# Three sealed experts, the last pair before expert work, V loaded once, and the zero fill spread over the pairs

## Chip, cores, metric

The kernel runs on one core of a Trainium2 chip. The metric is the device time in microseconds; the page and the trace come from one profiled execution, whose times are counted from its first instruction. The engines are named PE (matmul), PEld (its weight loads), DVE or VectorE, ACT or ScalarE, POOL or GpSimd, and SP or SyncE, which here only issues DMAs.

## What is computed

Attention in chunks over 4 batches, 8 heads, 768 positions, head size 64, then a top-2 mixture of 8 experts on the 3072 resulting rows of 512.

```python
for c in range(nc):                      # 24 chunks of 32 positions
    l_start = max(0, c_start - 16); r_end = min(S, c_end + 8)
    k_full = concat(mem_k, k[l_start:r_end]); v_full = concat(mem_v, v[l_start:r_end])   # 8 memory rows
    a = softmax(scale * q_c @ k_full.T); out[c] = a @ v_full
x = out as [3072, 512]
noisy_logits = x @ w_gate + log1p(exp(x @ w_noise)) * noise
top2, weights = the two largest of 8, softmax over them
for e in range(8): out[rows that chose e] += weight * (relu(x @ w1[e]) @ w2[e])          # 512 -> 1024 -> 512
```

## The kernel before

**Attention** runs over 16 pairs of heads (four pairs to a batch) in one software pipeline: iteration i of the main loop holds the steps of pairs i - 3 to i + 2. For a pair, q and k are turned by PE (`turn_pe`, copied out by ACT), scored (`scores_pe`), the maximum is taken off by VectorE (`max_dve`), ACT takes the exponent (`exp_act`), PE turns the result (`PT_pe`, copied by ACT in `PT_copy`), multiplies it with V (`PV_pe`), and VectorE normalises (`mult_dve`) into `xrows[b]`, a tile with all rows of batch b in two rotating buffers. `xT_pe` and `logits_pe` give the routing logits. q and k are loaded six pairs ahead. V is loaded three pairs ahead into four buffers `vbufs` (`load_v`): a chunk's window of 56 positions (16 left, 32 own, 8 right) lies on 56 partitions, so of 24 windows each position at an edge is loaded twice or more. These loads are issued by GpSimd, as they convert to bf16.

**Routing** of batch b (`route(b)`, steps s1 to s8) starts when the batch's logits are there: s1 the noise scale on ACT; s1b and s2 all-pairs comparison on VectorE; s2b, s2c masks and maxima; s2d exponent on ACT; s3 on PE the rank of each token in its expert, counted on from `seen`; s4 the weights and the store of `xrows[b]` to the DRAM tensor `x_rows` (SP's queue for batches 0 to 2, ACT's for 3); s4b, s5 slot and tile; s5c `col` on GpSimd; s5b `Rn` on VectorE; s6 the table by matmul; s7 adds the table of the batch before; s8 counts `seen` on. The steps of batches 0 to 2 are dealt out to the loop through `pending`, one group at each call of `steps`.

**Sealed slots.** Each expert has 7 tiles of 128 slots (the last 64). For the first EARLY experts, tiles 0 and 1 are filled from batches 0 and 1 alone, and tiles 2 and 3 from batches up to 2: in s8 the count is raised to the border (`gap`), and free slots are given to spare rows (`spare_a` to `spare_d`). So these tiles' tokens can be gathered before the last batch is routed: `begin_first` decodes the table after batch 1 and gathers tiles 0 and 1 (`idx_s`), after batch 2 follow tiles 2 and 3 (`idx_a`); everything else waits for the last table (`idx_f`, and `idx_h` for the half tiles).

**Expert work** is a generator, `every`: sets of an expert's tiles, in the order: the sealed tiles of the early experts in two halves (`part`: turn two tiles, then `up` over 256 slots), their `down`, then the remaining three tiles of each early expert, then the full experts. `gather` fetches a tile's rows by an indirect DMA of GpSimd; `turn` transposes them on PE; `up` is x @ w1 with ReLU on ACT and VectorE; `down` multiplies with w2, scales by the gate and scatters the result with addition into the output by an indirect DMA of GpSimd. The first scatter of a set waits for the landing of the whole set before it. Weights come in three buffers each, loaded by GpSimd between gathers and scatters. `units(k)` runs k steps of the generator between other work; `until` runs the rest.

In before, `every` starts in the main loop's iteration 15 and interleaves with the last pair (the loop has a 17th turn for it) and with the routing of batch 3. The output is zeroed by three DMAs on SP's queue after the loop.

The engines' queues are in program order, each engine on its own: an instruction that waits holds back everything behind it on its engine.

Of the kernel before, what the change touches and what calls it, by code (L numbers as in the profile page):

```python
# [12 lines left out]
F32 = mybir.dt.float32  # L13
BF16 = mybir.dt.bfloat16
# [10 lines left out]
def kernel(  # L25
# [14 lines left out]
    nc = tc.nc  # L40
# [12 lines left out]
    HP = H // 2  # L53
# [35 lines left out]
    def body():  # L89
# [27 lines left out]
        NQ = 6  # L117

        NV = 4
        vbufs = [ap_.tile([128, ncnk, 2, D], BF16, name=f"vp{i}", bufs=1) for i in range(NV)]  # L120

        def load_qk(n):
            b, h0 = divmod(2 * n, H)
# [4 lines left out]
        def load_v(n):  # L128
            vp = vbufs[n % NV]
            for hh in range(2):  # L130
                p0, hd = 64 * hh, 2 * n + hh

                def piece(c, m, j=0, nj=WIN):
                    nc.gpsimd.dma_start(  # L134
                        out=vp[p0 + j:p0 + j + nj, c:c + m, hh, :],
                        in_=bass.AP(v.tensor, v.offset + (hd * S + c * chunk + j - left_ctx) * D, [[D, nj], [chunk * D, m], [1, D]]))

                first, last = hd == 0, hd == B * H - 1
                if first:
                    piece(0, 1, left_ctx, WIN - left_ctx)  # L140
                if last:
                    piece(ncnk - 1, 1, 0, WIN - right_ctx)
                piece(int(first), ncnk - first - last)

        load_qk(0)
        identb = const.tile([128, 128], BF16, name="identb")
# [163 lines left out]
        def PV_pe(n):  # L310
            PT, vp = st[n]["PT"], vbufs[n % NV]
            pv = bankO[:, :, :UB * 2 * OW].rearrange("p x (u h c) -> p x u h c", h=2, c=OW)
            for u in range(BT):
                nc.tensor.matmul(out=pv[:, u // UB, u % UB], lhsT=PT[:, u, :], rhs=memv[:, n], start=(u % UB == 0), stop=False, skip_group_check=True)  # L314
            for c in range(ncnk):
                u, r = divmod(c, 4)
                nc.tensor.matmul(out=pv[32 * r:32 * r + 32, u // UB, u % UB, :, :D], lhsT=PT[:, u, 32 * r:32 * r + 32],  # L317
                                 rhs=vp[:, c], start=False, stop=True, skip_group_check=True)
            st[n]["po"] = pv

        def mult_dve(n):
# [32 lines left out]
        def route(b):  # L354
# [61 lines left out]
            def s4():  # L416
                ge, gs = R["ge"], T("gs", [128, BT])
                nc.vector.tensor_mul(ge, ge, R["two"])
# [3 lines left out]
                (nc.sync if b < B - 1 else nc.scalar).dma_start(out=xd_part[b][b * S:(b + 1) * S].rearrange("(t p) r -> p t r", p=128), in_=xrows[b])  # L422

            def s4b():
                sh = [128, BT, 2, E]
# [46 lines left out]
            def s8():  # L472
                if b == B - 1:
                    return
                sm = T("sm", [128, E])
                nc.vector.tensor_reduce(out=sm, in_=R["two"].rearrange("p t e -> p e t"), axis=AX, op=Alu.add)
# [4 lines left out]
                if b >= B - 3:  # L481
# [6 lines left out]
                    nc.vector.tensor_add(seen[:, :EARLY], seen[:, :EARLY], gap)  # L488

            if b == B - 1:  # L490
                return (s1,), (s1b, s2), (s2b, s3, s2c, s4b, s5, s5c), (s2d,), (s4, s5b), (s6, s7)
# [120 lines left out]
        def turn(s, j):  # L612
            e, tiles = sets[s]
            if s not in xTs:
                small = len(tiles) < NT
                xTs[s] = (mp if small else pools["full"]).tile([128, KP, SEALED * CAP if small else SLOTS], BF16, name="xTs" if small else "xTf", bufs=2)
                gts[s] = mp.tile([128, NT], F32, name="gt", bufs=4)
# [17 lines left out]
        def up(s, c0=0, c1=None):  # L635
            e, tiles = sets[s]
            c1 = total(s) if c1 is None else c1
            if s not in hts:
                small = len(tiles) < NT
                hts[s] = (mp if small else pools["full"]).tile([128, FB, SEALED * CAP if small else SLOTS], BF16, name="hts" if small else "htf", bufs=2)  # L640
            k = -(-(c1 - c0) // 512)
            for f in range(FB):
                for c in range(k):
                    h = hring[cnt["h"] % 3] if hring else tr()
# [46 lines left out]
        def every():  # L691
# [11 lines left out]
            def load(fn, e):  # L703
                return (lambda: fn(e),) if e < E else ()

            yield from down(0, load(load_w1, EARLY))
            gather(2 * EARLY, ALL, idx_f, load(load_w2, EARLY))
            yield from down(1)
            for s in range(EARLY, NS):
                e = sets[s][0]  # L710
                while todo and todo[0][0] <= s:
# [4 lines left out]
                        turn(*todo.pop(0))  # L716
                yield from up(s)
                if s == EARLY:
                    gather(2 * EARLY + 1, ALL, idx_f, load(load_w1, e + 3))
                elif s < NS - 1:  # L720
                    todo.extend((s + 1, j) for j in sets[s + 1][1])
                    yield from down(s - 1, load(load_w1, e + 3))
                    more = load(load_w2, sets[s - 1][0] + 3)
                    if s + 3 < NS:
                        gather(s + 3, ALL, idx_f, more)
                    else:
                        for fn in more:
                            fn()
# [26 lines left out]
        for i in range(NPAIR + 1):  # L755
            if i + NQ < NPAIR:
                load_qk(i + NQ)
            if i >= 1:
                PT_pe(i - 1)
            if i < NPAIR:  # L760
                max_dve(i)
            if i >= 1:
                PT_copy(i - 1)
            if i + 2 < NPAIR:
                turn_pe(i + 2, 0)
            if i < NPAIR:
                steps(1)
            if i >= 1:
                PV_pe(i - 1)
            if i < NPAIR:  # L770
                exp_act(i)
            if i >= 3:
                logits_pe(i - 3)
                if (i - 3) % HP == HP - 1:
                    begin, *rest = route((i - 3) // HP)
                    begin[0]()
                    assert not pending
                    pending.extend(rest)
# [4 lines left out]
            if i >= 2:  # L783
                xT_pe(i - 2)
            if i + 1 < NPAIR:
                scores_pe(i + 1)
# [6 lines left out]
            if i == NPAIR - 4:  # L793
                load_w1(1)
            if i == NPAIR - 2:
                load_w2(0)
            steps(1 if i < NPAIR - 2 else 2)
            if i >= NPAIR - 1:
                units(FB // 2)
        assert not pending  # L800
        pctx.close()
# [11 lines left out]
        logits_pe(NPAIR - 2)  # L813
        xT_pe(NPAIR - 1)
        cnt["by"] = "dve"
        for j in range(FIRST):
            turn(1, j)
        logits_pe(NPAIR - 1)
        begin, *rest = route(B - 1)
        begin[0]()  # L820
        units(3)
        cnt["by"] = "act"
        for g, more in zip(rest, (3, 4, 1, 4, 1)):
            for fn in g:
                fn()
            units(more)
# [135 lines left out]
```

## Time and profile before

| | us |
|---|---|
| median of 3 runs (342.05 to 343.34) | 343.24 |
| profiled execution | 343.07 |
| its span, first to last instruction | 341.3 |
| busy: PE / DVE / ACT / POOL | 274.3 / 161.2 / 149.5 / 229.3 |
| mean granted TensorE clock | 0.918 |

The span has three stages. Attention lasts to about 95, with the maximum of pair 12 at 79.45 and of pair 15 at 101.34. From there to 145 the last pair, the last routings and the first expert work share the engines. From 145 to 324 the experts run; the scatters and their landing end at 341.3. An idle time in brackets is what the engine waited before an instruction, and what ended the wait by the trace; "issue" is time in which it waited for nothing that the profile shows.

### The profile page before, as it was taken

To read this page: it belongs to the slowest core of one execution; us is meant where nothing else is said; L and a number is where in the kernel's file an instruction comes from. 1 tells how busy PE (TensorE), PEld (TensorE's weight loads), DVE (VectorE), ACT (ScalarE), POOL (GpSimd) and SP (SyncE) were. 2 spreads that over 40 slices of the span, in tenths; PEclk is the share of its full clock that TensorE was granted. 3 is DMA by queue.
4 is the path that set the end of the run, shared out by engine and by line. 5 is a ranking of instruction groups with operands and counts; after the bars stand their busy time and mean duration, and the time that the engine had idled before them with its cause. 6 is when DMAs were issued, how large, how long until landed. Compare 5 with 4: busy or idle time off the path is not lost. (4 is left out here: it accounts for less than half of the span.)

```text
span 341.3 us, 7625 instructions
## 1 busy us (share of the span) xinstructions
PE 274.3 (80%) x3071; PEld 174.2 (51%) x3085; DVE 161.2 (47%) x363; ACT 149.5 (44%) x295; POOL 229.3 (67%) x219
## 2 busy tenths in 40 slices
PE   0777677878548667799999999999999999999900
PEld 0656566666436555345565555555555555455400
DVE  7457659779876465222434333342332633134100
ACT  1688988878355544123343433423423333132200
POOL 8997767737443250687788887887888784848281
PEclk9969978969695999899999999999999999999965
DMA  9999999999979999469999999999999999959395
GB/s 108 161 154 187 167 161 166 212 133 194 196 143 309 398 286 203 79 103 185 247 152 198 172 240 197 239 195 194 206 160 205 216 148 157 147 74 130 40 131 70
DMA packets 99110, 60.30 MB, mean 177 GB/s; under 512 B 63488, under 2 KB 83968, under 8 KB 99072
## 3 DMA queue, kind: packets, MB, share of 16 engines
q0 software_dynamic: 82208, 49.84, 106.5%
q1 hardware_dynamic: 15792, 9.05, 9.2%
q10 hardware_dynamic: 1072, 0.88, 0.8%
q8 instruction: 26, 0.43, 0.5%
q14 instruction: 12, 0.10, 0.1%
HBM read 65.07 MB, written 23.27 MB: 259 GB/s over the span
## 5 line engine op out<-in xcount | busy, mean ns | idle before, releaser
L676 POOL DMA_INDIRECT out_dram<-ys,idx_f x40 | 62.8, 1570 | 26.6 <-issue 14.8
L648 PEld LDWEIGHTS <-w1t 128*128 128x128 bf16 x576 | 56.3, 99 | 40.4 <-issue 5.1
L604 POOL DMA_INDIRECT xl<-x_rows,idx_f x48 | 50.0, 1041 | 26.7 <-DVE hts L633 11.2
L664 PE MATMUL bankE<-w2t,htf 128*128 128x512 bf16 x278 | 65.7, 379 | 0.5
L675 DVE TENSOR_SCALAR ys<-bankE,gt 128x512 f32<-128x512 f32 (+1 forms) x32 | 21.9, 684 | 63.3 <-PE bankE L664 49.8
L648 PE MATMUL bankE<-xTf,w1t 128*128 128x416 bf16 x256 | 50.6, 339 | 0.0
L673 ACT ACTIVATE ys<-bankE,gt 128x512 f32<-128x512 f32 x24 | 16.5, 688 | 68.1 <-PE bankE L664 59.3
L134 POOL DMA_DIRECT2D vp<-in_v_dram x34 | 33.4, 989 | 15.5 <-PE bankO L317 4.3
L664 PEld LDWEIGHTS <-htf 128*128 128x128 bf16 x288 | 27.2, 98 | 28.8 <-issue 0.2
L633 DVE TENSOR_SCALAR htf<-bankE 128x416 bf16<-128x416 f32 x32 | 18.9, 591 | 26.7 <-PE bankE L648 26.7
L631 ACT ACTIVATE htf<-bankE 128x416 bf16<-128x416 f32 x32 | 16.5, 517 | 27.1 <-PE bankE L648 27.1
L264 ACT COPY kT<-bankT 64x768 bf16<-64x768 bf16 x32 | 25.3, 791 | 6.5 <-PE bankT L254 6.2
L648 PE MATMUL bankT<-xTf,w1t 128*128 128x416 bf16 x128 | 27.8, 339 | 0.2 <-DVE htf L633 0.2
L621 PE MATMUL bankT<-identb,xl 128*128 128x128 bf16 (+1 forms) x224 | 20.5, 220 | 5.7 <-DMA xl<-x_rows,idx_f 2.4
L621 PEld LDWEIGHTS <-xl 128*128 128x128 bf16 (+1 forms) x224 | 15.4, 100 | 16.2 <-issue 4.4
L664 PE MATMUL bankE<-w2t,hts 128*128 128x512 bf16 x92 | 22.7, 395 | 0.2
L288 DVE TENSOR_REDUCE mx<-bankS 128x12 f32<-128x768 f32 x16 | 15.2, 953 | 9.1 <-PE bankS L283 9.1
L314 PE MATMUL bankO<-memv,PT 128*128 128x132 bf16 x96 | 10.2, 256 | 9.5 <-ACT PT L307 9.3
L648 PE MATMUL bankE<-xTs,w1t 128*128 128x256 bf16 (+1 forms) x104 | 14.9, 283 | 2.6 <-DVE xTs L625 1.3
L456 POOL TENSOR_TENSOR col<-mm_all,tl 128x672 f16<-128x672 f16 x4 | 6.7, 1672 | 14.6 <-DVE tl L443 14.6
L329 DVE TENSOR_TENSOR xrow<-bankO,rec 128x768 bf16<-128x768 f32 x16 | 15.3, 958 | 1.9 <-DMA x_rows<-xrow 1.4
L290 DVE TENSOR_TENSOR sd<-bankS,mx 128x768 f32<-128x768 f32 x16 | 15.3, 958 | 1.8 <-DVE mx L288 0.5
(182 smaller groups left out, 453.6 us busy)
## 6 DMA issues: line engine op xcount, KB each, us to landing
w1t<-in_moe_w_dram POOLq DMA_DIRECT2D x8, 1024.0 KB, 11.3
w2t<-in_moe_w_dram POOLq DMA_DIRECT2D x8, 1024.0 KB, 10.7
out_dram<-zt SPq DMA_DIRECT2D x3, 2048.0 KB, 10.2
vp<-in_v_dram POOLq DMA_DIRECT2D x30, 168.0 KB, 8.6
qg<-in_q_dram POOLq DMA_DIRECT2D x16, 192.0 KB, 7.7
kg<-in_k_dram POOLq DMA_DIRECT2D x16, 192.0 KB, 8.2
x_rows<-xrow SPq DMA_DIRECT2D x3, 792.0 KB, 8.4
x_rows<-xrow ACTq DMA_DIRECT2D x1, 792.0 KB
```

What stands on the lines that cost most here:

```text
L134: nc.gpsimd.dma_start(out=vp[p0 + j:p0 + j + nj, c:c + m, hh, :], in_=bass.AP(v.tensor, v.offset + (hd * S + c * chunk + j - left_ctx) * D ...
L264: nc.scalar.copy(kbufs[n % 2][hs, hh].rearrange("d (p j) -> d p j", j=SJ), p_t[hs])
L290: nc.vector.tensor_tensor(out=sd, in0=st[n]["ps"], in1=mx.rearrange("p x (u o) -> p x u o", o=1).to_broadcast([128, 2, BT, CTX]), op=Alu.s ...
L604: nc.gpsimd.indirect_dma_start(out=xl, out_offset=None, in_=xd, in_offset=bass.IndirectOffsetOnAxis(ap=idx[:, c:c + 1], axis=0), bounds_ch ...
L621: nc.tensor.transpose(out=p_t[:, kp, :w], in_=xl[:w, kp * 64:(kp + 1) * 64].bitcast(BF16), identity=identb[:w, :w])
L631: nc.scalar.activation(out=dst, in_=src, func=Act.Relu)
L633: nc.vector.tensor_scalar(out=dst, in0=src, scalar1=0.0, scalar2=None, op0=Alu.max)
L648: nc.tensor.matmul(out=h[:, :hi - lo], lhsT=W1[e][:, kp, f * 128:(f + 1) * 128], rhs=xTs[s][:, kp, lo:hi], start=(kp == 0), stop=(kp == KP ...
L664: nc.tensor.matmul(out=y, lhsT=ht[:, f, o:o + w], rhs=W2[e][:, f, :], start=(f == 0), stop=(f == FB - 1))
L673: nc.scalar.activation(out=ys[:, :wide], in_=y[:, :wide], func=Act.Copy, scale=gate)
L675: nc.vector.tensor_scalar(out=ys[:, :wide], in0=y[:, :wide], scalar1=gate, scalar2=None, op0=Alu.mult)
L676: ins = nc.gpsimd.indirect_dma_start(out=rows, out_offset=bass.IndirectOffsetOnAxis(ap=idx, axis=0), in_=ys[:, :wide], in_offset=None, bou ...
```

## The change

- EARLY goes from 2 to 3: experts 0, 1 and 2 have sealed tiles, with three buffers for their turned rows and hidden values; sets are 11 instead of 10, and the order of gathers, weight loads and turns in `every` is adapted. W1 of expert 2 is loaded in pair 14, W1 of expert 1 in pair 11 instead of 12.
- `up` over 256 slots puts two blocks of 128 hidden units into one PSUM bank and evacuates both at once.
- The raising of the counts moves from s8 into a step s8b; for batch 1, s8 comes one group earlier.
- V is loaded once: 32 own positions of each chunk, as one contiguous row per partition; the left and right edges are then copied inside the SBUF by four DMAs of SP's queue a pair, which wait for the load.
- The zero fill is done in eight DMAs of SP's queue, in pairs 1 to 8, behind that pair's copies.
- The main loop ends with iteration 15. The steps of the last pair follow it, with the routing of batch 2 between them; expert work starts after the last pair's logits, in three portions of four units between the steps of the routings of batches 2 and 3. Batch 3's store goes to SP's queue.

```diff
-    EARLY = 2
+    EARLY = 3
...
         def load_v(n):
             vp = vbufs[n % NV]
             for hh in range(2):
-                p0, hd = 64 * hh, 2 * n + hh
...
+                p0, hd = 64 * hh + left_ctx, 2 * n + hh
+                nc.gpsimd.dma_start(
+                    out=vp[p0:p0 + chunk, hh],
+                    in_=bass.AP(v.tensor, v.offset + hd * S * D, [[D, chunk], [chunk * D, ncnk], [1, D]]))
+
+            for hh in range(2):
+                p0 = 64 * hh
+                nc.sync.dma_start(out=vp[p0:p0 + left_ctx, hh, 1:], in_=vp[p0 + chunk:p0 + chunk + left_ctx, hh, :ncnk - 1])
+                nc.sync.dma_start(out=vp[p0 + left_ctx + chunk:p0 + WIN, hh, :ncnk - 1], in_=vp[p0 + left_ctx:p0 + left_ctx + right_ctx, hh, 1:])
...
-                (nc.sync if b < B - 1 else nc.scalar).dma_start(out=xd_part[b]...
+                nc.sync.dma_start(out=xd_part[b]...
...
-                return (s1,), (s1b, s2), (s2b, s2c, s2d), (s3, s4, s4b, spare_a), (s5, s5c, spare_b), (s5b, spare_c), (s6, s7, s8, spare_d, begin_first)
+                return (s1,), (s1b, s2), (s2b, s2c, s2d), (s3, s4, s4b, spare_a), (s5, s5c, spare_b), (s5b, spare_c, s8), (s6, s7, s8b, spare_d, begin_first)
...
+            if 2 * w <= 512:
+                for f in range(0, FB, 2):
+                    h = hring[cnt["h"] % 3] if hring else tr()
...
+                    relu(hts[s][:, f:f + 2, c0:c1], h[:, :2 * w].rearrange("p (x w) -> p x w", w=w))
+                    yield "up", s, f
+                return
...
+            if 1 <= i <= 8:
+                zero_fill(NP // 8 * (i - 1), NP // 8)
...
+        n = NPAIR - 1
+        r2 = late[B - 2]
+        PT_pe(n)
+        PT_copy(n)
+        xT_pe(n - 2)
+        do(r2, "s1b", "s2")
+        PV_pe(n)
+        mult_dve(n)
+        logits_pe(n - 3)
+        xT_pe(n - 1)
+        logits_pe(n - 2)
...
+        do(r2, "s2b", "s2c")
+        xT_pe(n)
+        do(r2, "s3", "s4b", "s8")
+        logits_pe(n - 1)
+        turn(0, 0)
+        logits_pe(n)
+        r3 = route(B - 1)
+        do(r3, "s1")
+        do(r2, "s2d")
+        turn(0, 1)
+        do(r2, "s5", "s5c", "s8b", "s5b", "s4")
+        units(4)
+        do(r2, "s6", "s7")
         decode(tabs[(B - 2) % 2][:, :EARLY * NT], idx_a, None)
         for s in range(EARLY):
             gather(s, range(FIRST, SEALED), idx_a)
-        for x in range(3):
-            zero_fill(8 * x, 8)
         load_w2(1)
...
+        do(r3, "s1b", "s2", "s2b", "s2c")
+        units(4)
+        do(r3, "s3", "s4b", "s2d", "s5", "s5c", "s4", "s5b")
+        units(4)
+        do(r3, "s6", "s7")
...
         decode(tab, idx_f, idx_h)
         for s in range(EARLY, 2 * EARLY):
             gather(s, sets[s][1], idx_f)
-            todo.extend((s, j) for j in sets[s][1])
+        load_w2(2)
```

More of the change, by code (lines that the diff above doesn't have):

```diff
@@ L119, in body @@
         NV = 4
-        vbufs = [ap_.tile([128, ncnk, 2, D], BF16, name=f"vp{i}", bufs=1) for i in range(NV)]
+        vbufs = [ap_.tile([128, 2, ncnk, D], BF16, name=f"vp{i}", bufs=1) for i in range(NV)]
         def load_qk(n):
@@ L480, in s8, with s8b @@
                     nc.vector.tensor_copy(seen, sm)
-                if b >= B - 3:
+            def s8b():
+                if B - 3 <= b < B - 1:
                     ps_c = f32v(tr(), EARLY)
@@ L639, in up @@
                 small = len(tiles) < NT
-                hts[s] = (mp if small else pools["full"]).tile([128, FB, SEALED * CAP if small else SLOTS], BF16, name="hts" if small else "htf", bufs=2)
+                hts[s] = (mp if small else pools["full"]).tile([128, FB, SEALED * CAP if small else SLOTS], BF16, name="hts" if small else "htf", bufs=EARLY if small else 2)
             k = -(-(c1 - c0) // 512)
+            w = c1 - c0
+            if 2 * w <= 512:
+                for f in range(0, FB, 2):
+                    h = hring[cnt["h"] % 3] if hring else tr()
+                    cnt["h"] += 1
+                    for x in range(2):
+                        for kp in range(KP):
+                            nc.tensor.matmul(out=h[:, x * w:(x + 1) * w], lhsT=W1[e][:, kp, (f + x) * 128:(f + x + 1) * 128], rhs=xTs[s][:, kp, c0:c1],
+                                             start=(kp == 0), stop=(kp == KP - 1))
+                    relu(hts[s][:, f:f + 2, c0:c1], h[:, :2 * w].rearrange("p (x w) -> p x w", w=w))
+                    yield "up", s, f
+                return
             for f in range(FB):
@@ L704, in load @@
                 return (lambda: fn(e),) if e < E else ()
-            yield from down(0, load(load_w1, EARLY))
-            gather(2 * EARLY, ALL, idx_f, load(load_w2, EARLY))
-            yield from down(1)
+            for s in range(EARLY):
+                yield from down(s)
+                if s < EARLY - 1:
+                    for t in (EARLY,) if s == 0 else range(EARLY + s, 2 * EARLY):
+                        todo.extend((t, j) for j in sets[t][1])
             for s in range(EARLY, NS):
@@ L754, in body @@
                 scores_pe(0)
-        for i in range(NPAIR + 1):
+        late = {}
+        for i in range(NPAIR):
             if i + NQ < NPAIR:
@@ L782, in body @@
                 mult_dve(i - 1)
-            if i >= 2:
+            if 2 <= i < NPAIR - 1:
                 xT_pe(i - 2)
```

79 lines of the change are left out of this document (30 added, 49 removed).

## The prediction

> **What bounds the kernel now.** I read the table by stretches first, then GpSimd's timeline, then the groups, then the one place where VectorE waits for a DMA. The page's span line and four rows of the table by stretches (length; busy time and count of PE, PEld, DVE, ACT, POOL; granted clock; DMA share; GB/s):
>
> ```profile
> span 341.3 us, 7625 instructions
> 25.00:45.00 20.00, 15.09 (x408) 12.28 (x404) 12.61 (x18) 18.04 (x24) 14.43 (x17) 0.93 1.79 176
> 45.00:65.00 20.00, 14.96 (x371) 11.89 (x372) 16.92 (x37) 15.91 (x24) 15.07 (x17) 0.88 1.97 183
> 105.00:115.00 10.00, 7.04 (x87) 5.31 (x86) 4.90 (x13) 5.08 (x11) 2.76 (x1) 0.68 1.07 376
> 145.00:285.00 140.00, 137.68 (x891) 76.60 (x901) 51.93 (x102) 48.63 (x127) 111.14 (x90) 1.00 1.06 189
> ```
>
> In the attention stage (25 to 65) ACT is nearest to full (18.04 of 20 us), VectorE joins it once a batch is being routed (16.92), and DMA is busy in short pieces: 176 to 183 GB/s, where the zero fill of the output, nearly alone from 105 to 115, moves 376. In the expert stage PE is 98% busy, and GpSimd's 111 us hide gaps that its timeline shows (start, duration, idle before):
>
> ```profile
> 138.35 1.13 POOL L604 DMA_INDIRECT xl<-x_rows,idx_f  x1 [11.25 <-DVE hts L633]
> 285.93 1.59 POOL L676 DMA_INDIRECT out_dram<-ys,idx_f  x1 [4.74 <-DMA out_dram<-ys,idx_h]
> 302.67 1.55 POOL L676 DMA_INDIRECT out_dram<-ys,idx_f  x1 [4.03 <-DVE ys L675]
> 321.92 1.55 POOL L676 DMA_INDIRECT out_dram<-ys,idx_f  x1 [6.54 <-issue]
> 333.07 1.55 POOL L676 DMA_INDIRECT out_dram<-ys,idx_h  x1 [0.30 <-issue]
> L676 POOL DMA_INDIRECT out_dram<-ys,idx_f x40 | 62.8, 1570 | 26.6 <-issue 14.8 <-DMA out_dram<-ys,idx_h 4.7 <-DVE ys L675 4.3
> L604 POOL DMA_INDIRECT xl<-x_rows,idx_f x48 | 50.0, 1041 | 26.7 <-DVE hts L633 11.2 <-issue 9.4 <-PE bankT L621 1.2
> L557 POOL DMA_DIRECT2D w1t<-in_moe_w_dram x8 | 9.5, 1191 | 0.0
> L562 POOL DMA_DIRECT2D w2t<-in_moe_w_dram x8 | 8.4, 1053 | 0.0
> ```
>
> From 138.35 GpSimd issues without rest: a gather is 1.04 + 0.30 = 1.34 us, a scatter 1.57 + 0.30 = 1.87. 48 gathers (64.3), 56 scatters (104.7) and 12 weight loads (about 13.5) are 182.5; with the three waits (15.3, a set's first scatter waiting for the landing of the set before) that is 197.8, against 196.3 in the trace up to the last scatter's end at 334.62. Its landing ends the span. So GpSimd's queue sets the end, with PE close behind. Two numbers matter: the start S of the gathers by the final index table (138.35), and what is left for GpSimd and PE at S. S itself waits for data:
>
> ```profile
> 129.65 0.41 ACTq L422 DMA_DIRECT2D x_rows<-xrow  x1
> 133.83 0.23 DVE L549 TENSOR_SCALAR idx_h<-idx_f,halfc 128x8 int32<-128x8 int32 x1
> DMA to landing us min/median/max: 5.6/8.4/10.7
> ```
>
> The table is ready at 134; the store of the last batch's rows, issued at 129.65 (third row: all such stores), lands near 138. All sums below are made against the profiled execution: 343.07 us, 1.8 above its span and 0.2 below the median of the runs, 343.24.
>
> **The change part by part.** *Work ahead of S.* With three sealed experts 12 tiles instead of 8 are gathered before S, and one more W1 is loaded ahead: 4 x 1.34 + about 1.0 = 6.4 us leave GpSimd's queue after S. **-6.4.** The scatters stay 56.
>
> *What PE still owes at S.* Before S PE now does three of six half parts; the other three stand between the last table and the first down tile.
>
> ```profile
> 132.43 0.72 PE L621 MATMUL bankT<-identb,xl 128*128 128x128 bf16 x8
> 137.95 1.89 PE L664 MATMUL bankE<-w2t,hts 128*128 128x512 bf16 x7
> 150.54 7.08 PE L664 MATMUL bankE<-w2t,hts 128*128 128x512 bf16 x32
> L675 DVE TENSOR_SCALAR ys<-bankE,gt 128x512 f32<-128x512 f32 x24 | 18.0, 751 | 49.8 <-PE bankE L664 49.8
> ```
>
> One half part (turn two tiles, 32 matmuls) is 137.95 - 132.43 = 5.5 us, so three are 16.5. The table's last matmul lies 2.3 before S (below), so down starts at S + 14.2 and its first result is there at S + 14.2 + 1.9 + 0.75 = S + 16.8. GpSimd is ready at S + 9 gathers + one W2 = S + 13.4. It waits 3.4. Over the 12 tiles of these sets PE is as fast as GpSimd or a little slower: a tile is 7.08 / 4 = 1.77 against 1.87 for its scatter, but nine turns at 0.36 (half of the first row) lie between, so 0 to 2.1 more; I take 1. **+4.4.** Cover: none, since GpSimd sets the end. Evacuating two blocks of up at once (512 columns) I cost at nothing: a quarter of a half part gives 1.4 us for an evacuation that takes about 0.75 (last row); without that cover it would be the difference, four times a half part.
>
> *From the last pairs to S.* Now attention runs to its end, and the routings of batches 2 and 3 follow in turn. I count from the end of mult_dve(12), the normalisation of pair 12, which in before is at 93.29 (45.06 before S):
>
> ```profile
> 67.80 0.95 DVE L288 TENSOR_REDUCE mx<-bankS 128x12 f32<-128x768 f32 x1
> 92.33 0.96 DVE L329 TENSOR_TENSOR xrow<-bankO,rec 128x768 bf16<-128x768 f32 x1
> 98.41 0.20 DVE L369 TENSOR_TENSOR nl<-ns,nz_all 128x48 f32<-128x48 f32 x1
> 101.22 0.21 DVE L398 TENSOR_TENSOR gd<-nl,m 128x48 f32<-128x48 f32 x1
> 103.20 0.20 DVE L418 TENSOR_TENSOR ge<-ge,two 128x48 f32<-128x48 f32 x1
> 104.02 0.25 DVE L427 TENSOR_TENSOR rk<-mm_all,bankT 128x96 f32<-128x96 f16 x1
> 105.32 0.24 DVE L432 TENSOR_REDUCE r_all<-rk 128x12 f32<-128x96 f32 x1
> 106.66 1.75 DVE L450 TENSOR_TENSOR Rn<-rampm,slot 128x1536 f16<-128x1536 f16 x1
> 114.38 0.23 DVE L476 TENSOR_REDUCE sm<-two 128x8 f32<-128x48 f16 x1
> 115.59 0.16 DVE L488 TENSOR_TENSOR seen<-seen,gap 128x2 f16<-128x2 f16 x1
> 82.88 1.31 POOL L456 TENSOR_TENSOR col<-mm_all,tl 128x672 f16<-128x672 f16 x1 [1.38 <-DVE tl L443]
> 131.35 0.48 PE L463 MATMUL bankT<-col,Rn 128*128 128x56 f16 x12 [0.21 <-DVE Rn L450]
> ```
>
> VectorE has, up to the store of batch 2: two max-and-subtract pairs of two 0.96 steps (4.1), three normalisations (3.6), s1b to s2c (98.41 to 101.43: 3.0), s4 (0.8), rk (0.25), s5 (1.3), Rn (1.75), s8 and s8b (1.3): 16.1, and about 1 of waiting for PE and ACT. The store goes at +17 and lands at +24 (7, between 5.6 and 8.4). Six gathers wait for it: 8.0; then W2(1), 1.0 + 0.3; then batch 3's col, which stands behind these on GpSimd, 1.3; the table's matmuls 0.5; table and decoding 2.0 (131.83 to 133.83) + 0.3. Sum +37.4, against 45.06. **-7.7.** Batch 3's store is issued near +29 and lands inside that.
>
> *V once, copies and zero fill on SP.* A pair's V writes fall from 336 to 192 KB. Two chains grow. First, SP now waits for V to land before it copies its edges, and what stands behind waits too: the zero fill of the pair, and the store x_rows of batch 0 (issued in pair 7, after load_v(10)) and of batch 1 (pair 11, after load_v(14)). The xrow buffers are two, so mult_dve(8) and mult_dve(12) wait for those stores:
>
> ```profile
> 54.22 1.99 POOL L134 DMA_DIRECT2D vp<-in_v_dram  x2 [0.26 <-PE bankT L254]
> DMA to landing us min/median/max: 5.8/8.5/11.1
> 56.15 48.34 SPq L422 DMA_DIRECT2D x_rows<-xrow  x3
> 76.43 0.83 PE L317 MATMUL bankO<-vp,PT 128*32 128x128 bf16 x24
> 66.93 0.96 DVE L329 TENSOR_TENSOR xrow<-bankO,rec 128x768 bf16<-128x768 f32 x1 [1.39 <-DMA x_rows<-xrow]
> 77.58 1.98 POOL L134 DMA_DIRECT2D vp<-in_v_dram  x2 [3.18 <-PE bankO L317]
> 137.76 0.37 SPq L850 DMA_DIRECT2D gov<-x_rows  x1
> ```
>
> Already now the store of batch 0, issued at 56.15, holds mult_dve(8) until 66.93. After: V(10)'s second half is issued at 55.1 and lands at 62.6 (7.5, between least and median, as it is smaller); two copies and the zero fill issue first (three times 0.4), so the store goes at 63.8; the zero fill ahead of it takes 0.79 MB / 376 GB/s = 2.1, the store 8.4: 74.3. That is 7.4 later. From here to mult_dve(12) a pair takes (92.33 - 66.93) / 4 = 6.35, and in the next one VectorE itself needs 2.05 + 1.2 + 1.5 (half of s1b to s2c) = 4.75, so 1.6 comes back. **+5.8.** V(14): 78.5 + 7.5 + 0.8 + 6.5 (no zero fill ahead any more) = 93.3 against 92.33: **+1.0.** PV itself has room: V(10), issued at 54.22, is read at 76.43. Bounds: with least landings (55.1 + 5.8 + 1.2 + 2.1 + 5.6 = 69.8) the first costs 1.3 and the second nothing; with the largest (80.2; 101.1) 11.7 and 8.8. I stay near the middle.
>
> Second, 8 x 2.1 = 17 us of zero fill enter a stage whose DMA is busy, against 144 KB less V a pair, which at 183 GB/s is 0.8 us, 6 over the eight pairs. The net 11 us are a debt that the loads can carry: V has 22 us from issue to use and needs 11.1 at most, so 11 are free there, and q and k run six pairs ahead. The upper bound, with a third of it felt, is +4. The lower is -4: ACT idles 2 of 20 us in 25 to 45, and loads that come sooner can win no more than that over the loop's 40 us from 25. I take 0, between the two. In exchange the stretch after 105 is free of the fill.
>
> The Trainium skill, DMA: Bandwidth & Descriptors, section Issuing engines are not separate DMA queues, speaks against this part: whatever the issuing engine, all DMAs share the same 16 engines and interleave, so SP's queue adds no bandwidth. If by that rule none of the fill found room, the sum would be 17 higher. The trace agrees that the queues share (the store of batch 0 took 10.8 us to release its buffer beside loads, against 5.6 at the least), but it has no fill beside loads.
>
> **Sum:** -6.4 + 4.4 - 7.7 + 6.8 = -2.9: 343.07 - 2.9 = **340.2**.
>
> The skill's TensorE: Matmul & The Clock Gate, section What's actually happening, has a matmul clock that falls to half after an idle window of about 3.4 us and needs as long to return; PE would wait about 3 us for col before the last table, so the half parts would start at half speed: +1.7 by an estimate from that page, within my near sides. The trace agrees in kind: the granted clock is 0.68 in 105 to 115.
>
> **The rivals.** *A, slower: the stores held on SP decide.* Place: mult_dve(8) and mult_dve(12). For it: the stage's DMA is loaded (1.97) and now gets the zero fill, so landings near 11 rather than 8 are likely. Against: V is lighter. Midway between my value and the largest, the two cost 13.7 instead of 6.8: 347.1. The time is worse than before once they cost more than 9.7 together. *B, faster: the held stores cost little.* With least landings 1.3, and loads coming 1 sooner: 333.7. For it: less V traffic, and no zero fill beside the gathers of batch 2. *C, the routing does not get ahead:* six gathers stand in front of batch 3's col, and if batch 2's store takes 10.7 instead of 7, S comes 3.7 later: 343.9, no change. Against: zero fill is out of that stretch.
>
> **How the numbers follow.** About 0.5%, 1.7 us, is what a measurement of this kernel can tell from no change. Chances: my forecast with its near sides (336 to 341.3) 0.32; B 0.22; C 0.16; A 0.30. Faster 0.54, same 0.14 (C mostly), slower 0.32 (A and C's upper part). The range leaves out 0.1 on each side: 332 (B with another 1.5 from less DMA) to 349 (A with 2 more). The likely case alone spans 336 to 344.
>
> **What would show it.** In the new profile: mult_dve(8) with 8 to 9 us of waiting for x_rows in pair 9 and about 1 in pair 13; 15 to 18 us from mult_dve(12) to s4 of batch 2; the first idx_f gather about 37 us after mult_dve(12), near 137; 44 gathers behind it without rest; a first scatter that waits for ys. I am wrong if mult_dve(8) does not wait, if the attention loop itself is slower per pair in 30 to 60, or if GpSimd rests in the expert stage.

## The result, and the profile after

The changed kernel takes 365.8 us (median of 4 runs, 364.7 to 369.1) against 342.6 for the kernel before on the same chip: a ratio of 1.070, 95% interval 1.062 to 1.078. It is 7% slower where 0.8% faster was forecast, and beyond the upper end of the range, 349. The profiled execution took 364.7 us, 1.7 above its span of 363.0; the span is 21.7 longer than before.

The path of the prediction has three stretches. In the profiled executions:

| | before | forecast change | measured change |
|---|---|---|---|
| end of mult_dve(12) | 93.29 | +6.8 | +13.1 (106.41) |
| from there to S, the first idx_f gather | 45.06 | -7.7 | +3.1 (48.2) |
| from S to the end of the span | 202.95 | -6.4 + 4.4 | +5.5 (208.4) |

All three came out longer. The first, in VectorE's timeline (start, duration, idle before and its releaser):

```profile
59.53 0.96 DVE L325 TENSOR_TENSOR xrow<-bankO,rec 128x768 bf16<-128x768 f32 x1
78.87 0.96 DVE L325 TENSOR_TENSOR xrow<-bankO,rec 128x768 bf16<-128x768 f32 x1 [13.97 <-DMA x_rows<-xrow]
105.45 0.96 DVE L325 TENSOR_TENSOR xrow<-bankO,rec 128x768 bf16<-128x768 f32 x1 [2.41 <-DMA x_rows<-xrow]
```

Up to mult_dve(7) the loop keeps the pace of before (59.53 against 60.38). Then mult_dve(8) idles 14 us for the store of batch 0, where it waited 1.39 before. In the windows by stage (PE, PEld, VectorE, ACT, GpSimd busy, then clock, DMA share and GB/s) VectorE stands still for the whole stretch from 65 to 75. The GB/s at the ends of the first two rows are against 167 and 163 before:

```profile
35.00:45.00 10.00, 7.75 (x213) 6.07 (x211) 6.22 (x9) 8.51 (x12) 5.86 (x9) 1.00 1.42 275
45.00:55.00 10.00, 7.38 (x212) 5.84 (x209) 8.33 (x17) 8.42 (x15) 5.09 (x8) 1.00 1.42 262
65.00:75.00 10.00, 1.54 (x51) 1.33 (x48) 0.00 (x0) 3.85 (x6) 1.44 (x2) 0.71 1.40 281
```

SP's queue in the same place: the edge copies wait for V(10), which was issued near 53, then take 0.53 and 0.66 us each to issue; the fill and the store follow.

```profile
65.00 0.53 SPq L138 DMA_DIRECT2D vp<-vp  x1
65.59 0.66 SPq L139 DMA_DIRECT2D vp<-vp  x1
66.36 0.53 SPq L138 DMA_DIRECT2D vp<-vp  x1
66.93 0.66 SPq L139 DMA_DIRECT2D vp<-vp  x1
67.63 0.44 SPq L575 DMA_DIRECT2D out_dram<-zt  x1
68.57 0.38 SPq L418 DMA_DIRECT2D x_rows<-xrow  x1
```

The V loads' own answer for 35 to 72 gives their time to landing, which was 7.9/8.9/10.6 before, for 168 KB a load instead of 96:

```profile
DMA to landing us min/median/max: 8.4/10.5/15.4
```

The second stretch, in the timelines of GpSimd, VectorE and SP:

```profile
131.44 1.11 POOL L602 DMA_INDIRECT xl<-x_rows,idx_a  x1 [10.55 <-DVE rk L423]
133.40 0.21 DVE L417 TENSOR_TENSOR xrow<-ge,gs 128x48 f32<-128x48 f32 x1
139.10 1.01 POOL L602 DMA_INDIRECT xl<-x_rows,idx_a  x1 [0.30 <-issue]
140.10 0.97 POOL L560 DMA_DIRECT2D w2t<-in_moe_w_dram  x1
142.08 0.37 SPq L418 DMA_DIRECT2D x_rows<-xrow  x1
154.59 1.11 POOL L602 DMA_INDIRECT xl<-x_rows,idx_f  x1 [12.17 <-DMA x_rows<-xrow]
```

and a line of SP's waits (total, times, longest):

```profile
SPq L418 <- DMA xl<-x_rows,idx_a: 17.9, 3, 11.7
```

Batch 3's rows are ready at 133.6, but their store is issued at 142.08: it waits until the idx_a gathers, which read the same DRAM tensor, have landed. Behind W2(1) it then needs 12 us more, and S waits for that. In the kernel before, the last of these gathers was issued at 120.88 and the four took 6.3 to 7.6 us to land, so all had landed before the last store was due (129.65). The dependency cost nothing there and I passed it over.

The third stretch, the first scatters of the sealed sets, and the end; the first row is the first scatter of set 1 in the kernel before, where seven gathers stood ahead of it:

```profile
166.40 1.63 POOL L676 DMA_INDIRECT out_dram<-ys,idx_a  x1 [0.30 <-issue]
167.48 1.64 POOL L686 DMA_INDIRECT out_dram<-ys,idx_a  x1 [0.30 <-issue]
182.85 1.56 POOL L686 DMA_INDIRECT out_dram<-ys,idx_a  x1 [8.13 <-DVE xTs L623]
194.82 1.56 POOL L686 DMA_INDIRECT out_dram<-ys,idx_a  x1 [4.82 <-DVE hts L631]
355.09 1.55 POOL L686 DMA_INDIRECT out_dram<-ys,idx_h  x1 [0.30 <-issue]
```

Between sets 0, 1 and 2 no gathers stand any more, so a set's first scatter sits out the landing of the set before: 8.13 + 4.82 us, new. (The engines named in the brackets had long been done.)

### The profile page after: what moved, and what is told of

It is laid out like the page before. It is cut to its first block, busy times and chain, and to the rows that moved or that the text cites. A ratio compares the mean times of both kernels' runs of the same rounds, so it can differ in the third digit from the quotient of the medians.

```text
span 363.0 us, 7817 instructions
## 1 busy us (share of the span) xinstructions
PE 278.5 (77%) x3103; PEld 179.1 (49%) x3117; DVE 160.3 (44%) x354; ACT 149.1 (41%) x288; POOL 218.0 (60%) x217
## 3 DMA queue, kind: packets, MB, share of 16 engines
q1 hardware_dynamic: 18192, 12.13, 11.6%
## 5 line engine op out<-in xcount | busy, mean ns | idle before, releaser
L686 POOL DMA_INDIRECT out_dram<-ys,idx_f x36 | 56.6, 1572 | 23.9 <-issue 13.0
L674 PE MATMUL bankE<-w2t,htf 128*128 128x512 bf16 x232 | 54.6, 379 | 0.8 <-issue 0.4
L658 PEld LDWEIGHTS <-w1t 128*128 128x128 bf16 x416 | 40.3, 98 | 29.3 <-issue 1.7
L658 PE MATMUL bankE<-xTf,w1t 128*128 128x416 bf16 x216 | 43.4, 342 | 0.4 <-DVE htf L631 0.4
L132 POOL DMA_DIRECT2D vp<-in_v_dram x32 | 23.3, 733 | 29.6 <-PE bankL L343 16.8
L674 PE MATMUL bankE<-w2t,hts 128*128 128x512 bf16 x138 | 33.4, 391 | 0.8 <-DMA w2t<-in_moe_w_dram 0.6
L686 POOL DMA_INDIRECT out_dram<-ys,idx_a x12 | 18.8, 1566 | 16.0 <-DVE xTs L623 8.1
L647 PEld LDWEIGHTS <-w1t 128*128 128x128 bf16 x192 | 20.6, 109 | 10.5 <-issue 3.3
L658 PE MATMUL bankT<-xTf,w1t 128*128 128x416 bf16 x104 | 22.5, 339 | 0.0
L291 ACT ACTIVATE P<-sd 128x768 bf16<-128x768 f32 x16 | 13.6, 848 | 21.8 <-DVE sd L286 21.8
L674 PEld LDWEIGHTS <-hts 128*128 128x128 bf16 x144 | 13.9, 100 | 16.0 <-issue 1.3
## 6 DMA issues: line engine op xcount, KB each, us to landing
w2t<-in_moe_w_dram POOLq DMA_DIRECT2D x8, 1024.0 KB, 11.3
```

Source lines behind the costliest of these rows:

```text
L132: nc.gpsimd.dma_start(out=vp[p0:p0 + chunk, hh], in_=bass.AP(v.tensor, v.offset + hd * S * D, [[D, chunk], [chunk * D, ncnk], [1, D]]))
L647: nc.tensor.matmul(out=h[:, x * w:(x + 1) * w], lhsT=W1[e][:, kp, (f + x) * 128:(f + x + 1) * 128], rhs=xTs[s][:, kp, c0:c1], start=(kp == ...
L658: nc.tensor.matmul(out=h[:, :hi - lo], lhsT=W1[e][:, kp, f * 128:(f + 1) * 128], rhs=xTs[s][:, kp, lo:hi], start=(kp == 0), stop=(kp == KP ...
L674: nc.tensor.matmul(out=y, lhsT=ht[:, f, o:o + w], rhs=W2[e][:, f, :], start=(f == 0), stop=(f == FB - 1))
L686: ins = nc.gpsimd.indirect_dma_start(out=rows, out_offset=bass.IndirectOffsetOnAxis(ap=idx, axis=0), in_=ys[:, :wide], in_offset=None, bou ...
```

## The experiments

Theories at the start: T1, the store held on SP makes the loop late; T2, the store of batch 3 waiting for the idx_a gathers makes S late; T3, the landing waits between the sealed sets are empty GpSimd time. Rival to T1: R1, the zero fill loads the DMA queues for everyone. All runs in one table, from one profiled execution each; the ratio is from the repeated runs, to the kernel before on the same chip. The execution of c1_again was one of its longest (354.8 us against a median of 351.7), that of c2_split one of its shortest (344.1 against 347.8):

| run | mult_dve(12) ends | S | S to the end | span | ratio (95%) |
|---|---|---|---|---|---|
| before | 93.3 | 138.4 | 203.0 | 341.3 | |
| changed | 106.4 | 154.6 | 208.4 | 363.0 | 1.070 (1.062 to 1.078) |
| e1_third | 92.4 | 148.6 | 209.1 | 357.7 | 1.050 (1.044 to 1.057) |
| e2_late | 102.0 | 151.7 | 209.4 | 361.1 | 1.054 (1.045 to 1.062) |
| e3_view | 105.5 | 145.5 | 212.8 | 358.3 | 1.043 (1.032 to 1.054) |
| e4_fill | 105.7 | 155.6 | 203.2 | 358.8 | 1.051 (1.044 to 1.059) |
| e5_fillafter | 92.1 | 143.6 | 209.0 | 352.6 | 1.043 (1.030 to 1.056) |
| e6_fillinloop | 104.5 | 145.5 | 205.8 | 351.3 | 1.023 (1.016 to 1.031) |
| e7_vonce | 97.5 | 141.8 | 204.9 | 346.7 | 1.015 (1.006 to 1.024) |
| c1_all | 93.2 | 135.8 | 204.1 | 339.9 | 0.994 (0.989 to 0.999) |
| c1_again | 92.0 | 146.6 | 206.3 | 352.9 | 1.011 (1.007 to 1.015) |
| c2_split | 91.0 | 135.9 | 206.2 | 342.1 | 0.998 (0.995 to 1.002) |
| e8_noview | 90.6 | 141.4 | 204.4 | 345.8 | 1.001 (0.997 to 1.004) |
| c3_vthird | 92.8 | 143.7 | 205.6 | 349.3 | 1.004 (1.002 to 1.007) |

**A third row buffer** (it borrows the buffer of W2(2)):

```
-xrows[b] = ap_.tile([128, BT, ROW], I32, name="xrow", bufs=2)
+if b == 2:
+    spare_w2 = w2p.tile([128, FB, Dm], BF16, name="w2t")
+    xrows[b] = ...   # its first bytes, viewed as rows
+else:
+    xrows[b] = ap_.tile([128, BT, ROW], I32, name="xrow", bufs=2)
```

> The changed kernel, but batch 2's rows have a third buffer (they lie in the buffer that W2(2) takes later), so that mult_dve(8) and mult_dve(12) overwrite nothing that a store still reads. The stores stay where they are on SP. T1 (the two stores held on SP behind the V copies cost the loop 13.1 us): neither mult waits for x_rows, mult_dve(12) ends near 93.5 instead of 106.4, and the whole is 11 to 13 us shorter: 353 to 355. Rival R1 (the loop is slower because zero fill and copies load the DMA queues, and the waits for x_rows only show it first): other loads come late in their place, V or q and k, mult_dve(12) ends after 100, the whole gains under 6: over 360.

T1 is right on the loop and wrong on the end: mult_dve(12) ends 14.0 sooner, yet the whole gains 4.7. The fill is still in the pairs and V still takes 10.4 us to land (10.5 in the changed kernel), so R1 as it stands here falls: the longer landings do not slow the loop by themselves, only through a store that holds one of two buffers. The timelines show where the rest of the gain went:

```profile
91.42 0.96 DVE L329 TENSOR_TENSOR xrow<-bankO,rec 128x768 bf16<-128x768 f32 x1
113.00 0.37 SPq L422 DMA_DIRECT2D x_rows<-w2t  x1
126.81 1.11 POOL L606 DMA_INDIRECT xl<-x_rows,idx_a  x1 [12.64 <-DMA x_rows<-w2t]
```

Batch 2's store now goes out at 113.00, right behind W1(2) and W2(0) (111.0, 111.8), and takes 13.8 us until the gathers may start; in the changed kernel it came 9 us after those loads and took 7.8.

**Copies a pair later:** `edges_v(n)`, the four copies, called one pair after `load_v(n)`.

> The changed kernel, but SP issues the edge copies of V(n) one pair later, when V(n) has landed; two row buffers as before, zero fill as in the change. T1 (the order on SP: the store stands behind copies that wait for a landing): store of batch 0 is issued near 57 instead of 68.6 and lands 8 to 10 us later, mult_dve(8) goes near 67, mult_dve(12) ends at 93 to 96, the whole is 10 to 13 shorter: 353 to 356. R1 (the load of the DMA queues): the store is issued early but lands 12 us or more later, mult_dve(8) goes after 70, and the gain is under 8.

R1 is the nearer one: the store is issued at 64.5 (not 57, not 68.6) and holds mult_dve(8) until 75.87. V takes 12 us to land, two pairs, so the copies still wait; and the store itself takes 11. The order on SP is worth some 4 of the 13 us.

**Gathers that wait for three stores only:**

```
-    out=xl, ..., in_=xd, ...
+    out=xl, ..., in_=xd_part[B] if idx is idx_a else xd, ...
+if idx is idx_a: ...   # waits for the stores of batches 0 to 2
```

> The changed kernel, but the six idx_a gathers are made to wait for the stores of batches 0 to 2 alone (they read no row of batch 3), so that the store of batch 3 need not wait until they have landed. T2 (that wait makes S late): the store is issued near 134 instead of 142.1, lands by 145, S (the first idx_f gather) comes with the table instead, 147 to 148 instead of 154.6. But PE has its first result of down only near 164.3, whatever S is, so the first scatter moves from 167.5 only to 164.4: the whole is about 3 shorter, 362 to 363. Rival R2 (the store lands late because six gathers and W2(1) share the DMA queues with it): S comes after 151 and the whole moves by less than 1.5.

```profile
122.47 8.71 SPq L419 DMA_DIRECT2D x_rows<-xrow  x2
145.53 1.11 POOL L603 DMA_INDIRECT xl<-x_rows,idx_f  x1 [3.15 <-DVE idx_h L548]
164.34 1.64 POOL L690 DMA_INDIRECT out_dram<-ys,idx_a  x1 [6.22 <-DVE ys L689]
```

T2's rows are there: the store of batch 3 goes out at 130.8 (the first line spans the stores of batches 2 and 3), S waits for the table and comes 9.1 sooner, the first scatter at 164.34 waits 6.22 us for ys, as the prediction's PE term had it, and the span is 4.7 shorter. But the edit takes two things away at once. The store also stands 9 us ahead of W2(1) now (140.08) and lands within 4.0 us; in the changed kernel it stood 2.0 behind that load and took 12.0. By an estimate from these rows, a landing of 4.0 after the issue at 142.08 would alone have brought S to 146.6, one later than here. So the run does not part T2's wait from R2's landing, and by this estimate the late S needs both.

**Gathers of set 6 between the sealed sets:**

```
 if s < EARLY - 1:
+    gather(2 * EARLY, range(3) if s == 0 else ALL, idx_f)
```

> The changed kernel, but the seven gathers of set 6 (the first whole expert) are issued between the scatters of the sealed sets: three after set 0, four after set 1, instead of after up of set 3. T3 (GpSimd sets the end from S on, and the waits of 8.1 and 4.8 us for the landing of the sealed sets' scatters are empty time that gathers can fill): the two waits shrink to about 4 and 0, nothing of the seven gathers (9.2 us) stands later, and the whole is 8 to 9 shorter: 356 to 358. Rival R3 (PE sets the end, or the landings come later by as much as gathers stand beside them): the gain is under 3.

```profile
183.96 1.63 POOL L686 DMA_INDIRECT out_dram<-ys,idx_a  x1 [4.17 <-DMA out_dram<-ys,idx_a]
196.89 1.63 POOL L686 DMA_INDIRECT out_dram<-ys,idx_a  x1 [0.30 <-issue]
210.04 1.60 POOL L686 DMA_INDIRECT out_dram<-ys,idx_f  x1 [5.05 <-DMA out_dram<-ys,idx_a]
```

The two waits shrink to 4.17 us and to the usual 0.30, 8.8 less together. But the gathers that moved had covered the landing of set 2, and set 3's first scatter now waits 5.05 for it. 4.4 us gained, half of what was expected: T3 holds, with one more boundary than I counted.

**Zero fill out of the pairs:** the fill is placed as before, behind the store of batch 2; store of batch 3 on ACT's queue.

> The changed kernel without zero fill in the pairs: the three fills of 2 MB stand on SP behind the store of batch 2, as in the kernel before, and the store of batch 3 goes on ACT's queue, as there. V once, the copies and two row buffers stay. R1 as the last runs left it (copies held by V landings of 10 to 13 us, and these are long because the fill loads the DMA queues): V lands within 8.5, the store of batch 0 is issued by 64, lands by 72, mult_dve(8) goes near 72 instead of 78.9, mult_dve(12) ends at 97 to 100, and the whole, with the fills beside batch 2's gathers again (0 to 3 later there), is 4 to 8 shorter: 358 to 362. T1 (the order on SP alone): mult_dve(8) stays after 76, the gain is under 2, or it is slower.

```profile
DMA to landing us min/median/max: 3.1/4.7/5.8
```

```profile
58.46 0.39 SPq L418 DMA_DIRECT2D x_rows<-xrow  x1
91.15 0.96 DVE L325 TENSOR_TENSOR xrow<-bankO,rec 128x768 bf16<-128x768 f32 x1 [2.88 <-DMA x_rows<-xrow]
```

The first line is of the V loads from 35 to 72, the others are of the timelines. Without the fill they land in 4.7 instead of 10.5, the store goes out 10 us sooner, mult_dve(8) waits for nothing, and mult_dve(12) ends 14.3 sooner, 1.2 before the old kernel. R1 in this form is shown, beyond what it expected. The fill then costs beside batch 2's gathers (ACT waits 13.72 us for one of them), so 10.4 remain in the span. Either edit, the third buffer or the fill taken out, gives back the whole loop: the delay needs long landings and a store that holds a buffer, both.

**The fill alone**, on the kernel before:

> The kernel before, with the zero fill in pairs 1 to 8 on SP (eight times 0.75 MB) instead of behind the store of batch 2; nothing else of the change. R1 (the fill loads the queues for everyone): the store of batch 0 is issued near 57 but lands 13 to 15 us later, mult_dve(8) goes at 70 to 72 instead of 66.9, V and q and k land in 11 to 13, and the whole is 2 to 6 slower than before: 346 to 350. T1 (only the order on SP behind the copies matters): mult_dve(8) within 1.5 us of before, and the whole the same or up to 3 faster, since the gathers of batch 2 have the queues for themselves.

```profile
51.19 0.83 PE L317 MATMUL bankO<-vp,PT 128*32 128x128 bf16 x24 [10.21 <-DMA vp<-in_v_dram]
103.58 0.96 DVE L329 TENSOR_TENSOR xrow<-bankO,rec 128x768 bf16<-128x768 f32 x1
```

The loop loses 11.3 us, more than expected, and at another place: one V load in 35 to 72 took 20.8 us to land and PV itself waited 10.2 for it. Of this 7.5 reach the end. But this run does not spread the fill as the change does. Here SP's queue holds no copies that wait for a landing, and SP's timeline has seven of the eight fills between 22.95 and 37.12, the eighth at 65.92; in the changed kernel they go out one by one from 33.71 to 73.33. The median V load landed in 8.9 us, as before. So the run shows what a burst of fills costs, and not what the spread fill costs when V is loaded whole.

**V once alone**, on the kernel before:

> The kernel before, with V loaded once and its edges copied on SP; zero fill, routing and experts as before. T1 (the order on SP): the store of batch 0 waits behind copies that wait for V(10), is issued near 62 instead of 56.2, lands near 70, mult_dve(8) goes 3 to 4 later and a part of it comes back: 1 to 4 slower than before, 345 to 348. R1 (the load): V once has fewer packets and, copies included, as many bytes (192 + 138 KB a pair against 336), so V lands in 6 to 7 and the store by 68: within 1 of before, or faster.

mult_dve(8) waits 0.32 and starts at 65.0; R1 is right there. But mult_dve(12) waits 6.53 for the store of batch 1. It goes out at 84.97, behind V(14)'s copies, 5.6 later than before: T1 at one place. And it holds the buffer for 11.6 us, with 1 MB of W1(1) issued 1.6 ahead of it; in e5_fillafter, with that load 9 us ahead, it is 7.3. The whole is 1.5% slower.

**Five edits together:** the third buffer, the free gathers, set 6's gathers moved, batch 3's `col` on VectorE, and W1(2), W2(0) to W2(2) moved away from batch 2's store.

> The changed kernel with five edits together: a third row buffer; the idx_a gathers free of batch 3's store; set 6's gathers between the sealed sets' scatters; batch 3's col on VectorE instead of GpSimd; W1(2) loaded in pair 12, W2(0) behind the idx_a gathers, W2(1) and W2(2) among the idx_f gathers, so that batch 2's store lands beside no weights. If the three delays are what was found (row buffers, the chain store-gathers-store, empty landing waits) and W loads were what took back the gain of the third buffer: mult_dve(12) ends at 92 to 93, batch 2's store lands within 8, S at 129 to 132, the first scatter at 144 to 147 instead of 167.5, and the whole is 337 to 342, within 2% of before on either side or faster. If instead DMA load or PE takes it back, the first scatter comes after 152 and the whole stays above 347.

```profile
108.80 0.83 PE L313 MATMUL bankO<-vp,PT 128*32 128x128 bf16 x24 [4.29 <-DMA vp<-vp]
119.32 0.37 SPq L423 DMA_DIRECT2D x_rows<-w2t  x1
123.90 1.37 POOL L607 DMA_INDIRECT xl<-x_rows,idx_a  x1 [6.26 <-DVE df L378]
135.78 1.09 POOL L607 DMA_INDIRECT xl<-x_rows,idx_f  x1 [1.78 <-DVE xTs L631]
151.71 1.63 POOL L694 DMA_INDIRECT out_dram<-ys,idx_a  x1 [2.29 <-DVE ys L693]
```

25 us of the changed kernel's time go: the three delays, with the weight loads that they ran into, together account for its loss on this chip. The share of each of the five edits is not shown. Batch 2's store has landed 4.6 us after its issue. S and the first scatter are 4 to 5 later than hoped, since pair 15 waits 4.29 for V's copies behind the W loads. A second time, on another chip:

> The kernel with five edits once more, beside the kernel before on the same chip: a second time 0 to 1.2% faster than before if its first ratio, 0.994, was no accident of one chip; 1.0 or above if it was.

1.011 (1.007 to 1.015): slower there, so it is not shown to be faster than the kernel before. Its profiled execution differs from that of c1_all in the order of two transfers:

```profile
133.34 0.98 POOL L565 DMA_DIRECT2D w2t<-in_moe_w_dram  x1
135.09 0.37 SPq L423 DMA_DIRECT2D x_rows<-xrow  x1
146.07 0.36 SPq L894 DMA_DIRECT2D gov<-x_rows  x1
```

The load of `gov` reads all of x_rows, so its issue marks the landing of batch 3's store. Here the rows are ready at 135.06, W2(0) has gone out 1.8 us ahead of the store, and the store lands after 11.0 us; S is 146.6. In c1_all the store went out at 130.50, 2.5 ahead of W2(0), landed after 4.7, and S is 135.8.

**V(15) ahead of W1(1), fill split,** and the same without the free gathers:

> The kernel with the five edits together, with two more: W1(1) and W1(2) are both loaded in pair 12 behind V(15) (in the run with five edits PV of pair 15 waited 4.3 us for V's copies, V(15) having landed 16.6 us after its issue behind W1(1)), and the zero fill is split: two blocks of 128 rows in each of pairs 1 to 8 instead of three, four in each of pairs 13 and 14, behind V(15)'s copies. If DMA load ahead of the last V was what held the last pair: no wait of PV, the last normalisation ends near 105 instead of 110.9, S near 131 instead of 135.8, the whole 335 to 338. If the fill in pairs 13 and 14 holds the stores of batches 1 and 2 instead: S at 135 or later, the whole 339 or more.

> The kernel of the run before this one, but with the idx_a gathers reading the whole of x_rows again, so that the store of batch 3 waits until they have landed. T2: with the other delays gone this wait is no longer covered by PE: the store of batch 3 is issued 8 us later, S comes 7 to 9 us later, and of that 4 to 8 reach the end (PE's first result of down leaves GpSimd little room). R2 (PE sets the first scatter anyway): under 3.

c2_split: the last normalisation came at 105.1 as expected, but S stayed at 135.9, and the time did not fall. The second branch's cause is not there either: the gathers started 4.6 us after batch 2's store. What holds S there stays open. e8_noview has S 5.5 later and a span 3.7 longer, while the ratios overlap: not settled which of T2 and R2 holds there. Their rows show the same order of store and load again, c2_split first, then e8_noview:

```profile
128.70 0.37 SPq L423 DMA_DIRECT2D x_rows<-xrow  x1
131.23 0.98 POOL L565 DMA_DIRECT2D w2t<-in_moe_w_dram  x1
133.37 0.36 SPq L895 DMA_DIRECT2D gov<-x_rows  x1
```

```profile
128.06 0.98 POOL L564 DMA_DIRECT2D w2t<-in_moe_w_dram  x1
129.90 0.37 SPq L422 DMA_DIRECT2D x_rows<-xrow  x1
140.84 0.36 SPq L891 DMA_DIRECT2D gov<-x_rows  x1
```

With 1 MB of W2(0) issued 2.5 us behind the store, it landed after 4.7. With the load issued 1.8 ahead of it, it took 10.9. In e8_noview the rows are ready at 128.90, so the wait for the gathers held the store by only 1.0; its landing beside the load took 6.3 more. All of these are single executions.

**V once with a third buffer,** on the kernel before:

> The kernel before, with V once (edges copied on SP) and the third row buffer; zero fill, routing and experts as before. If the held store was the only cost of V once (in the run with V once alone mult_dve(12) waited 6.5 us for it, and the loop had no other loss): mult_dve(12) ends near 91 instead of 93.3, S 2 to 3 before 138.35, the whole 1 to 4 shorter than before. If V once costs elsewhere too (copies that PV waits for, stores that the gathers wait for): no change, or slower by up to 3.

The loop is as expected (92.8), but S comes at 143.7, waiting for the store of batch 3, which went out on ACT's queue at 131.10, behind the fill and W2(1), and landed after 12.0 us; before, it went out at 129.65 and took 8.1. The kernel is 0.4% slower: the two edits have a cost beyond the held store, and these runs do not show which of them has it.

## Why the prediction was wrong, step by step

**The zero fill's debt (0, -4 to +4) is the term that was furthest off.** I reckoned that V had 11 us of slack and q and k six pairs, so longer landings would be borne. V, q and k did bear them in the changed kernel, where PV waits for no V; the copies and the store behind them on SP did not. Taking the fill out is worth 14.3 us at mult_dve(12) in e5_fillafter. It acts only through the stores that hold the two buffers: with a third one the loop ends at 92.4 with the fill in place (e1_third). So this term and the next can't be added up one by one. I had also taken 144 KB less V a pair, but the edge copies write it back (2 x 46 + 2 x 23 = 138 KB, and 192 + 138 = 330 against 336), so nothing made room. The Trainium skill's rule that I set against this part (DMA: Bandwidth & Descriptors, Issuing engines are not separate DMA queues: all DMAs share the same 16 engines) gave 17 more than my sum, 357. The trace agrees that they share: 4.7 against 10.5 us to landing without and with the fill. The 17 itself, a fill that finds no room, is not borne out: the stretch from 35 to 65 moved 251 to 275 GB/s with the fill and 157 to 182 without. That 357 lies nearer to 364.7 than my sum is in part luck.

**The held stores (+6.8)** were the right mechanism at the right two places, mis-sized: +13.1. I took 7.5 for V(10) to land (the copies that wait for it start at 65.00, near 12) and three issues of 0.4 ahead of the store; it was four copies and the fill, 3.6 us from 65.00 to 68.57. Without the fill the same order costs from less than nothing (e5_fillafter: -1.2) to 4.2 (e7_vonce). Rival A named the places and nearly the price (13.7); it ended at 347 because it moved only this term.

**Routing (-7.7)** has the largest miss of the three stretches. It failed by a dependency that I had before me in the waits of SP's queue and did not weigh. Batch 2's store went at +17.2 (forecast +17) and its gathers at +25.0 (+24); batch 3's store at +35.7 instead of +29. I had put the landing of that store at nothing; it took 12.0, behind W2(1). With both gone, S is 40.0 after mult_dve(12) in e3_view, against the forecast 37.4. Rival C expected S late from the gathers ahead of `col`; `col` did run at 141.06, but the table was not what S waited for.

**Work ahead of S (-6.4)** is there: 44 gathers remain behind S. **PE's debt (+4.4)** was hidden while S was late: the first scatter follows the gathers without a wait; e3_view shows it, S + 18.8 against the forecast S + 16.8. PE also restarts at a lower granted clock after its wait for `col` (0.70 from 145 to 155, 1.00 from 155 to 165):

```profile
142.47 0.72 PE L459 MATMUL bankT<-col,Rn 128*128 128x56 f16 x12 [6.17 <-POOL col L452]
145.94 3.60 PE L647 MATMUL bankE<-xTs,w1t 128*128 128x256 bf16 x16 [1.05 <-DVE xTs L623]
149.33 1.88 PE L647 MATMUL bankT<-xTs,w1t 128*128 128x256 bf16 x8
155.03 1.91 PE L647 MATMUL bankE<-xTs,w1t 128*128 128x256 bf16 x16
```

The same 16 matmuls take 1.7 us more, and the next 8 take 1.88 where 8 such matmuls later take 1.04, 0.8 more. In the changed kernel these 2.5 us lay beside the wait for the store. The estimate from the clock gate's page of the Trainium skill (TensorE: Matmul & The Clock Gate, What's actually happening) was 1.7: the trace agrees in kind, and its 2.5 is larger.

**The landing waits between the sealed sets** I left out: "44 gathers behind it without rest" was the sign I gave, and they came, but none between sets 0, 1 and 2. -6.4 and 8.13 + 4.82 make +6.6, against the measured +5.5.

The three misses, +6.3, +10.8 and +7.5, make the whole difference of 24.6 between 340.2 and 364.7.

**Open:** why c1_all is 0.6% faster on one chip and 1.1% slower on another. The order of one store against one load is worth 6 us in these rows, and the one trace of c1_again has the slower order; whether its other executions have it too, and what delays the store there, is not shown.

## What to carry to other kernels

Slack is to be checked for every reader of a loaded transfer, not only for the one that the transfer was meant for: here the loads' consumers had room and a store two steps behind them on the same queue had none. When steps are put closer together or in a new order, list for each store who still reads the same tensor, and for each set boundary what filled the wait for the landing; a dependency that costs nothing before may be the next chain. Lines moved to the same place in the program go out at other times when nothing on their queue waits, so the issue times of a control are to be read before its result is used. An edit that frees time in one stretch moves its transfers next to others, so the gain is to be forecast at the next landing, not at the freed instruction.

## What the runs showed of the hardware

With eight fills of 0.75 MB, one a pair, the stretch from 35 to 65 moved 251 to 275 GB/s in the changed kernel instead of 157 to 182 in e5_fillafter, and a 96 KB load took 10.5 us to landing instead of 4.7: throughput up by half, latency doubled. A store of 792 KB landed in 4.0 to 4.7 us in the three traces in which GpSimd issued 1 MB of weights 2.5 us or more behind it (e3_view, c1_all, c2_split), and in 10.9 to 12.0 us in the six in which it issued them 1.8 to 2.3 us ahead (the changed kernel, e1_third, e2_late, e4_fill, e8_noview, c1_again).
